# Opening SyncE's queue with wq and the K chunks, and loading x from ScalarE's queue, in a decode kernel of cached attention and a token mixer

## The chip, the cores and the metric

The kernel runs on one core of one Trainium2 chip. The core has TensorE (PE in the profile, with PEld for its weight loads), VectorE (DVE), ScalarE (ACT), GpSimd (POOL) and SyncE (SP), which here does nothing but issue DMAs. The metric is the device time of one execution in microseconds; less is better.

## The reference

Two layers, each a block of grouped-query attention over a cache and a token-mixing MLP, both with a residual. There are 2 batch rows with one token each and 512 channels; 32 query heads share 8 heads of keys and values, each with a cache of 32768 positions of 128 floats. Cut to what matters:

```python
def _A_ref(x, k_cache, v_cache, wq, wo):
    q = (x @ wq).reshape(B, Sq, Hq, Dh).transpose(0, 2, 1, 3)
    scores = jnp.einsum("bhqd,bhkd->bhqk", q, jnp.repeat(k_cache, rep, axis=1)) * (Dh ** -0.5)
    p = softmax(scores)
    o = jnp.einsum("bhqk,bhkd->bhqd", p, jnp.repeat(v_cache, rep, axis=1))
    return o.transpose(0, 2, 1, 3).reshape(B, Sq, Hq * Dh) @ wo

def _B_ref(x, w1, b1, w2, b2):           # S = 1 token, F = 1792
    u = gelu(jnp.einsum("bsd,sf->bdf", x, w1) + b1)     # x is layernormed again inside
    return jnp.einsum("bdf,fs->bds", u, w2) + b2

x = A_x
for _ in range(2):                        # the same weights and caches in both layers
    x = x + _A_ref(layernorm(x), k_cache, v_cache, wq, wo)
    x = x + _B_ref(layernorm(x), w1, b1, w2, b2)
```

All is float32. The caches are 2 x 8 x 32768 x 128 floats each for K and V, 268 MB each, and both layers read them whole.

## The kernel before, in words

The work is cut into 32 units: a layer, a batch row and one of the 8 heads of the cache. A unit reads its part of K and then of V in 8 chunks each; a chunk is a tile of 128 partitions by 4096 floats, 2 MB. All chunks, of K (`k_chunk`, L180) and of V (`v_chunk`, L247), are loaded from SyncE's queue into one ring of three buffers (`ring`, tile `chunk`). A load is issued as soon as the instructions that read the buffer's last content are done.

The order of the program is written out by hand (`manual_schedule`): a loop over slots (L412) that in each slot issues one chunk of K of a unit and one chunk of V of the unit before, and around them the small steps that two dictionaries, `pre` and `post`, assign to slots. Each engine runs its own instructions in that order, and each queue issues its DMAs in that order.

A unit's steps:

- `make_q` (L162): 16 products of a 128x128 block of wq with a column of the layernormed x (`xnT`); VectorE copies the four query vectors into `qpad`.
- `k_chunk`: scores of a chunk, 8 products with 512 positions each (L193; in float32 each counts as two matmuls in the profile); after each fourth chunk VectorE transposes the scores and takes the maximum.
- `max_1`, `max_2`: the maximum over the unit, and exp on ScalarE (L232).
- `v_chunk`: products of the weights with V, accumulated in `acc` (L270).
- `out_1`, `out_2`: sum, division, and the products with wo, added into `rows`.

After the last unit of a layer and a row come the mixer (`mix_2`, `mix_3`, `mix_3_out`) and `mix_4`, which adds to `xrow` and, in the last layer, issues the output row from ScalarE's queue (L366). `cols_sb` holds w1, b1, w2 and b2; the mixer alone reads it.

What concerns the change is the start. VectorE clears the tile `xrow` (L66), whose partitions 0 and 32 then receive the two rows of x (L68), 2 KB each. wq and wo are cut by head into 8 tiles each of 1 MB; `load_wq(0)` (L78, the DMA itself in L73) comes before the loop, the others in slots of the loop: wq of head 1 in slot 2, behind the third K chunk. From ScalarE's queue `cols_sb` is loaded (L80). Then VectorE and GpSimd prepare constants (VectorE: `selg`, `acc`, `rows`; L95 to L107). Before the loop stand the steps of the first unit: `attention_input` (L138) layernorms `xrow` with VectorE and GpSimd (L114 to L118), `to_columns` (L144) turns each row into columns by products with the identity (L149) and copies (L153), and `make_q(0, r)` forms the first q (L168, L176). Then the loop begins with chunk 0 of K. The chunks 0, 1 and 2 find empty buffers; chunk 3 takes the buffer of chunk 0.

Of the kernel before, what the change touches and what calls it, by code (L numbers as in the profile page):

```python
# [8 lines left out]
F32 = mybir.dt.float32  # L9
# [4 lines left out]
P = 128  # L14
# [16 lines left out]
def gqa_mixer_kernel(ctx: ExitStack, tc: tile.TileContext, x, kt, v, wq, wo, cols, out):  # L31
# [9 lines left out]
    nc = tc.nc  # L41
    B, D = x.shape
# [12 lines left out]
    const = ctx.enter_context(tc.tile_pool(name="const", bufs=1))  # L55
# [6 lines left out]
    ctx.enter_context(tc.manual_schedule())  # L62


    xrow = const.tile([P, D], F32, name="xrow")
    nc.vector.memset(xrow, 0.0)  # L66
    for b in range(B):
        nc.sync.dma_start(xrow[32 * b : 32 * b + 1, :], x[b : b + 1, :])  # L68
    wq_sb = [const.tile([P, DT, R * DH], F32, name=f"wq{h}") for h in range(HKV)]
    wo_sb = [const.tile([P, R, D], F32, name=f"wo{h}") for h in range(HKV)]  # L70

    def load_wq(h):
        nc.sync.dma_start(wq_sb[h].rearrange("p t c -> p (t c)"), wq[h])  # L73
# [2 lines left out]
        nc.sync.dma_start(wo_sb[h].rearrange("p t c -> p (t c)"), wo[h])  # L76

    load_wq(0)  # L78
    cols_sb = const.tile([P, 3 * FT + 1], F32, name="cols_sb")
    nc.scalar.dma_start(cols_sb, cols)  # L80
    w1c, b1c, w2c = (cols_sb[:, k * FT : (k + 1) * FT] for k in range(3))
# [74 lines left out]
    def unit_of(n):  # L156

        return units[n]
# [217 lines left out]
    for n in range(NU):  # L376
        layer, b, h = unit_of(n)
# [93 lines left out]
```

## Time and profile before

| | us |
|---|---|
| median of 3 runs | 2580.58 (2580.49 to 2580.9) |
| profiled execution | 2582.35 |
| its span, first to last instruction | 2580.6 |
| PE busy | 1676.7 (65%) |
| DVE busy | 224.1 (9%) |
| ACT busy | 135.3 (5%) |

In all 1085.71 MB move, at a mean of 421 GB/s over the span; 1084.27 MB of them belong to q1, the queue of SyncE. q10 is ScalarE's. TensorE was granted 0.788 of its clock in the mean.

In the views that follow, a row of the timeline has the start, the time that the instructions took, the engine (SPq and ACTq are the queues of SyncE and ScalarE that issue DMAs), the line and the operation, and behind them what ended an idle time before. A row of windows has, for each stretch, its length, the busy time and count of instructions of PE, PEld, DVE, ACT and POOL, then the granted clock of TensorE, the mean busy share of the 16 DMA engines and the GB/s. A row of a DMA queue has the number of packets, the MB and the share of the 16 engines' time. A row of DMA issues has the size of each transfer and the time from issue to landing.

### The profile page before, as it was taken

To read this page: it belongs to the slowest core of one execution; us is meant where nothing else is said; L and a number is where in the kernel's file an instruction comes from. 1 tells how busy PE (TensorE), PEld (TensorE's weight loads), DVE (VectorE), ACT (ScalarE), POOL (GpSimd) and SP (SyncE) were. 2 spreads that over 40 slices of the span, in tenths; PEclk is the share of its full clock that TensorE was granted. 3 is DMA by queue.
4 is the path that set the end of the run, shared out by engine and by line. 5 is a ranking of instruction groups with operands and counts; after the bars stand their busy time and mean duration, and the time that the engine had idled before them with its cause. 6 is when DMAs were issued, how large, how long until landed. Compare 5 with 4: busy or idle time off the path is not lost.

```text
span 2580.6 us, 22231 instructions
## 1 busy us (share of the span) xinstructions
PE 1676.7 (65%) x10088; PEld 488.4 (19%) x10088; DVE 224.1 (9%) x473; ACT 135.3 (5%) x280; POOL 7.0 (0%) x21
## 2 busy tenths in 40 slices
PE   6565666566676666765765666667667667667655
PEld 3111112121211221211211211212212212112111
DVE  1000000000021000000000000002001100000002
ACT  0000000000010000000000000001000100000001
POOL 0000000000000000000000000000000000000000
PEclk8877777777787778788778788878787877777887
DMA  9999999999999999999999999999999999999995
GB/s 404 428 427 427 428 426 428 426 427 425 427 427 426 423 426 421 427 428 427 427 426 427 425 428 425 427 426 428 425 428 421 426 428 427 428 427 425 428 428 220
DMA packets 76710, 1085.71 MB, mean 421 GB/s; under 512 B 8644, under 2 KB 8644, under 8 KB 9032
## 3 DMA queue, kind: packets, MB, share of 16 engines
q1 hardware_dynamic: 76468, 1084.27, 99.1%
q8 instruction: 79, 1.29, 0.2%
q14 instruction: 15, 0.12, 0.0%
q10 hardware_dynamic: 148, 0.03, 0.0%
HBM read 1084.25 MB, written 0.00 MB: 420 GB/s over the span
## 4 chain that ended last, share of the span: by engine, by line
DMA 77%; PE 22%; DVE 1%; issue 1%; ACT 0%; POOL 0%; POOLq 0%; SPq 0%; DVEq 0%; ACTq 0%
DMA chunk<-in_kt_dram 39%; DMA chunk<-in_v_dram 38%; PE acc L270 10%; PE scores L193 10%; PE misc L168 1%; PE misc L284 0%; PE rows L299 0%; DVE chunk L335 0%; PE rows L350 0%; PE misc L149 0%; PE misc L282 0%; ACT chunk L343 0%; ACT S L232 0%; DVE ln_st L114 0%; PE bcast L318 0%
## 5 line engine op out<-in xcount | busy, mean ns | idle before, releaser
L193 PE MATMUL scores<-chunk,qpad 128*32 128x512 f32 x4096 | 687.4, 803 | 457.5 <-DMA chunk<-in_kt_dram 455.0
L270 PE MATMUL acc<-chunk,S 128*16 128x512 f32 x4000 | 679.8, 811 | 421.8 <-DMA chunk<-in_v_dram 419.7
L193 PEld LDWEIGHTS scores<-chunk,qpad 128*32 128x32 f32 x4096 | 133.2, 128 | 887.5 <-DMA chunk<-in_kt_dram 452.5
L270 PEld LDWEIGHTS acc<-chunk,S 128*16 128x16 f32 x4000 | 109.1, 110 | 843.0 <-DMA chunk<-in_v_dram 586.1
L232 ACT ACTIVATE S<-S,neg 128x256 f32<-128x256 f32 x128 | 95.3, 749 | 2257.9 <-DVE neg L228 2257.9
L168 PEld LDWEIGHTS misc<-xnT,wq 128*128 128x128 f32 x1024 | 152.9, 230 | 157.9 <-issue 157.9
L168 PE MATMUL misc<-xnT,wq 128*128 128x1 f32 x1024 | 163.4, 281 | 0.0
L204 DVE STREAM_TRANSPOSE S<-scores 128x512 f32<-128x512 f32 x64 | 45.9, 717 | 845.6 <-PE scores L193 845.6
L176 DVE COPY qpad<-misc 128x4 f32<-128x4 f32 x32 | 5.2, 162 | 796.0 <-PE misc L168 796.0
L205 DVE TENSOR_REDUCE mx<-S 128x4 f32<-128x512 f32 x64 | 67.9, 1061 | 2.2
L284 PE MATMUL misc<-selg,row 128*128 128x4 f32 x256 | 42.2, 288 | 1.0 <-DVE row L280 1.0
L284 PEld LDWEIGHTS misc<-selg,row 128*128 128x128 f32 x256 | 40.7, 241 | 1.2 <-DVE row L280 1.2
L299 PE MATMUL rows<-wo,oT 128*1 128x512 f32 x256 | 40.0, 695 | 0.5 <-DVE oT L294 0.5
L220 DVE TENSOR_REDUCE m<-misc 4x1 f32<-4x128 f32 x32 | 8.9, 279 | 241.3 <-PE misc L218 241.3
L343 ACT ACTIVATE hid<-hid 128x2048 f32<-128x2048 f32 (+1 forms) x12 | 20.4, 1697 | 119.0 <-DVE hid L335 119.0
L280 DVE COPY row<-acc 128x512 f32<-128x512 f32 x32 | 21.8, 680 | 36.4 <-PE acc L270 36.4
L335 DVE TENSOR_SCALAR hid<-row,cols_sb 128x512 f32<-128x512 f32 x42 | 20.2, 541 | 53.4 <-PE rows L350 53.4
L232 ACT ACTIVATION_READ_ACCUMULATOR S<-S,neg 128x1 f32 x128 | 23.9, 187 | 0.0
L292 DVE RECIPROCAL rl<-misc 128x4 f32<-128x4 f32 x32 | 5.8, 182 | 170.9 <-PE misc L284 170.9
L282 PEld LDWEIGHTS misc<-lsum,one 128*128 128x128 f32 x64 | 12.3, 241 | 42.2 <-issue 42.2
L270 PE MATMUL acc<-kept,S 128*16 128x512 f32 x96 | 17.2, 840 | 2.1 <-DMA kept<-in_v_dram 2.1
L224 PEld LDWEIGHTS misc<-ident,m 4*128 4x128 f32 x64 | 11.2, 217 | 39.2 <-issue 38.3
(50 smaller groups left out, 193.6 us busy)
## 6 DMA issues: line engine op xcount, KB each, us to landing
chunk<-in_kt_dram SPq DMA_DIRECT2D x256, 2048.0 KB, 12.1
chunk<-in_v_dram SPq DMA_DIRECT2D x247, 2048.0 KB, 12.6
wq<-in_wq_dram SPq DMA_DIRECT2D x8, 1024.0 KB, 15.4
wo<-in_wo_dram SPq DMA_DIRECT2D x8, 1024.0 KB, 14.8
chunk<-in_v_dram SPq DMA_DIRECT2D x5, 1024.0 KB, 10.2
kept<-in_v_dram SPq DMA_DIRECT2D x2, 2048.0 KB, 16.4
kept<-in_v_dram SPq DMA_DIRECT2D x2, 1024.0 KB, 13.9
chunk<-in_v_dram SPq DMA_DIRECT2D x1, 512.0 KB, 11.1
```

The source lines that it names most:

```text
L168: nc.tensor.matmul(q_ps[n][:, r : r + 1], wq_sb[h][:, d, r * DH : (r + 1) * DH], xnT[layer, b][:, d : d + 1], start=(d == 0), stop=(d == D ...
L193: nc.tensor.matmul(sc_ps[n][32 * g : 32 * g + 32, :], q, kc[:, (k * NG + g) * w : (k * NG + g + 1) * w], start=(i == 0 and k == 0), stop=( ...
L204: nc.vector.transpose(S[n][:, half, :], sc_ps[n])
L205: nc.vector.tensor_reduce(mx[n][:, half, :], S[n][:, half, :].rearrange("p (t h) -> p h t", h=R), axis=AX.X, op=ALU.max,)
L232: nc.scalar.activation(s[:, :, h], s[:, :, h], AF.Exp, bias=neg[:, h : h + 1], scale=SCALE, accum_out=lsum[n][:, h : h + 1],)
L270: nc.tensor.matmul(acc[32 * g : 32 * g + R * QT, :], S[n][:, half, col : col + R * QT], (own if q < stay else vc)[:, q * w : (q + 1) * w], ...
L280: nc.vector.tensor_copy(asb, acc)
L282: nc.tensor.matmul(po[:, R : 2 * R], ones, lsum[n], start=True, stop=True)
L284: nc.tensor.matmul(po[:, :R], asb[:, t * DH : (t + 1) * DH], selg[:, t * R : (t + 1) * R], start=(t == 0), stop=(t == QT - 1),)
L299: nc.tensor.matmul(rows[b][32 * r : 32 * r + 1, :], oT[n][:, r : r + 1], wo_sb[h][:, r, :], start=(units[n] == lay[layer, b][0]), stop=(un ...
L335: nc.vector.tensor_scalar(u[:, k * D : (k + 1) * D], hx[key], w1c[:, f : f + 1], b1c[:, f : f + 1], op0=ALU.mult, op1=ALU.add,)
L343: nc.scalar.activation(u[:, : n * D], u[:, : n * D], AF.Gelu_apprx_tanh)
```

## The change

The two tile lists and the two loading functions move up, so that `load_wq(0)` is the first DMA in SyncE's order. The memset of `xrow` keeps its place on VectorE. The two rows of x are issued from ScalarE's queue, ahead of `cols_sb`. SyncE's queue then holds wq of head 0, the K chunks 0, 1 and 2, wq of head 1 and chunk 3, with no transfer of x among them. Sizes, tiles and all else stay.

```diff
+    wq_sb = [const.tile([P, DT, R * DH], F32, name=f"wq{h}") for h in range(HKV)]
+    wo_sb = [const.tile([P, R, D], F32, name=f"wo{h}") for h in range(HKV)]
+
+    def load_wq(h):
+        nc.sync.dma_start(wq_sb[h].rearrange("p t c -> p (t c)"), wq[h])
+
+    def load_wo(h):
+        nc.sync.dma_start(wo_sb[h].rearrange("p t c -> p (t c)"), wo[h])
+
+    load_wq(0)
     xrow = const.tile([P, D], F32, name="xrow")
     nc.vector.memset(xrow, 0.0)
     for b in range(B):
-        nc.sync.dma_start(xrow[32 * b : 32 * b + 1, :], x[b : b + 1, :])
-    wq_sb = [const.tile([P, DT, R * DH], F32, name=f"wq{h}") for h in range(HKV)]
-    wo_sb = [const.tile([P, R, D], F32, name=f"wo{h}") for h in range(HKV)]
...
-    load_wq(0)
+        nc.scalar.dma_start(xrow[32 * b : 32 * b + 1, :], x[b : b + 1, :])
     cols_sb = const.tile([P, 3 * FT + 1], F32, name="cols_sb")
     nc.scalar.dma_start(cols_sb, cols)
```

More of the change, by code (lines that the diff above doesn't have):

```diff
@@ L62, in gqa_mixer_kernel @@
     ctx.enter_context(tc.manual_schedule())
[L65 to L68, printed above, removed]
     wq_sb = [const.tile([P, DT, R * DH], F32, name=f"wq{h}") for h in range(HKV)]
@@ L78, in gqa_mixer_kernel @@
     load_wq(0)
+    xrow = const.tile([P, D], F32, name="xrow")
+    nc.vector.memset(xrow, 0.0)
+    for b in range(B):
+        nc.scalar.dma_start(xrow[32 * b : 32 * b + 1, :], x[b : b + 1, :])
     cols_sb = const.tile([P, 3 * FT + 1], F32, name="cols_sb")
```

## The prediction

> **What bounds the kernel now.** I read the page from the top: the span, the busy shares, the row of the DMA in 40 slices, then the chain that ended last.
>
> ```profile
> span 2580.6 us, 22231 instructions
> PE 1676.7 (65%) x10088; PEld 488.4 (19%) x10088; DVE 224.1 (9%) x473; ACT 135.3 (5%) x280; POOL 7.0 (0%) x21
> DMA  9999999999999999999999999999999999999995
> DMA 77%; PE 22%; DVE 1%; issue 1%; ACT 0%; POOL 0%; POOLq 0%; SPq 0%; DVEq 0%; ACTq 0%
> ```
>
> The DMA is at nine tenths or more in 39 of 40 slices and carries 77% of the chain; the busiest engine, PE, has 65%. To see whether the DMA ever rests, I cut the span in three windows. The last two columns are the DMA's busy share and GB/s.
>
> ```profile
> 0.00:3.00 3.00, 0.00 (x0) 0.00 (x0) 1.84 (x5) 1.28 (x1) 0.95 (x10) 1.00 0.06 9
> 3.00:2550.00 2547.00, 1660.65 (x10024) 484.86 (x10028) 209.13 (x441) 126.13 (x274) 4.95 (x9) 0.79 1.01 426
> 2550.00:2580.60 30.60, 16.08 (x68) 3.58 (x60) 13.15 (x28) 7.85 (x5) 1.10 (x2) 0.76 0.02 6
> ```
>
> From 3 to 2550 us the transfers run without rest (share 1.01, 426 GB/s). So the kernel is a dead start of 3 us, a stream of fixed length, and a serial tail of 30 us. A microsecond gained or lost where the stream starts is kept to the end, because no slack lies in the stream that could swallow it. A change that touches only the start has to be read in the first 25 us, in SyncE's queue first.
>
> ```profile
> SPq L68 <- DVE xrow L66: 0.7, 1, 0.7
> ...
> 1.43 0.63 SPq L68 DMA_DIRECT2D xrow<-in_x_dram  x2
> 2.11 0.35 SPq L73 DMA_DIRECT2D wq<-in_wq_dram  x1
> 2.50 1.66 SPq L184 DMA_DIRECT2D chunk<-in_kt_dram  x3
> 4.21 0.45 SPq L73 DMA_DIRECT2D wq<-in_wq_dram  x1
> 20.04 3.97 SPq L184 DMA_DIRECT2D chunk<-in_kt_dram  x3
> ```
>
> SyncE waits 0.7 us for VectorE's memset of xrow (L66), spends 0.63 us on the two rows of x and issues wq at 2.11. After three K chunks and the second wq the ring of three buffers is full, and the fourth chunk goes out at 20.04, when PE has read the first. That PE work hangs on x:
>
> ```profile
> 0.74 0.39 ACTq L80 DMA_DIRECT2D cols_sb<-in_cols_dram  x1
> 0.91 0.48 DVE L66 MEMSET xrow<- 128x512 f32 x1 [0.91 <-PEq L457]
> 1.17 1.28 ACT L232 ACT_TABLE_LOAD   x1 [1.17 <-PEq L457]
> 2.34 1.03 DVE L107 MEMSET rows<- 128x512 f32 x2
> 3.29 0.69 DVE L114 BATCH_NORM_STATS2 ln_st<-xrow 128x6 f32<-128x512 f32 x1
> 9.17 6.97 PE L168 MATMUL misc<-xnT,wq 128*128 128x1 f32 x32
> 16.17 0.16 DVE L176 COPY qpad<-misc 128x4 f32<-128x4 f32 x1 [6.66 <-PE misc L168]
> 16.43 7.19 PE L193 MATMUL scores<-chunk,qpad 128*32 128x512 f32 x48 [0.30 <-issue]
> ```
>
> x, layernorm, columns, q, scores are one serial line from 3.29 to 20.04, with no wait for a transfer in it before the third chunk. So there are two clocks at the start: when the stream begins, and when x's line frees the first buffer. The change moves the first earlier and perhaps the second later.
>
> **The change, part by part.**
>
> *SyncE's queue opens with wq.* Its first DMA no longer waits for the memset nor stands behind the two issues of x. The wait of 0.7 us ended at 1.43, so SyncE was ready at 0.73; ScalarE's first issue at 0.74 shows the same start. wq moves from 2.11 to 0.74, and the three chunks and the second wq with it: the stream begins 1.37 us earlier. That is −1.37 us at the end if nothing runs dry.
>
> *x on ScalarE's queue.* The issue still waits for the memset (0.91 plus 0.48), so it begins at 1.43 as before. Behind it on ScalarE stand cols and the table load. cols goes out about 1.3 us later and the table load ends near 3.8 instead of 2.45. They are covered, and I take them at nothing:
>
> ```profile
> 60.06 0.77 ACT L232 ACTIVATE S<-S,neg 128x256 f32<-128x256 f32 x1 [57.61 <-DVE neg L228]
> 749.06 0.99 DVE L335 TENSOR_SCALAR hid<-row,cols_sb 128x512 f32<-128x512 f32 x2
> ```
>
> The table is first used at 60.06 and cols at 749.06; without that cover they would cost at most the 1.3 us each.
>
> *x now travels beside the stream.* Before, it went ahead of wq on idle DMA engines. Its last packet, the completion write of the second row, is the one packet of q1 in the window 2.8 to 3.0 us:
>
> ```profile
> q1 hardware_dynamic: 1, 0.00, 0.3%
> ```
>
> VectorE was busy with memsets until just before 3.29, so x may land 0.3 us later for nothing. How late it lands under load is seen nowhere at the start; the nearest rows are those of the first output row, also 2 KB, also from ScalarE's queue, in the full stream. The fence gives ScalarE's issue, SyncE's own issues around it, the landing of the chunk issued just ahead of it (11.0 us), and the packets of queue q10 in the windows 2039.65 to 2039.75 and 2040.35 to 2040.45, and of q1 in the 0.6 us between:
>
> ```profile
> 2036.19 0.49 ACTq L366 DMA_DIRECT2D out_dram<-xrow  x1
> ...
> 2033.67 0.33 SPq L261 DMA_DIRECT2D chunk<-in_v_dram  x1
> 2036.93 0.33 SPq L184 DMA_DIRECT2D chunk<-in_kt_dram  x1
> ...
> chunk<-in_v_dram SPq DMA_DIRECT2D x1, 2048.0 KB, 11.0
> ...
> q10 hardware_dynamic: 1, 0.00, 5.4%
> ...
> q1 hardware_dynamic: 16, 0.26, 102.3%
> ...
> q10 hardware_dynamic: 1, 0.00, 0.6%
> ```
>
> The row's data moved 3.5 us after its issue and its completion write 4.2 us after. It didn't wait for the chunk issued at 2033.67, which landed at 2044.7: it got between that chunk's packets. Sixteen engines moved sixteen packets of 16 KB in the 0.6 us between its two packets, one each. So a small transfer here waits some microseconds and then takes turns one for one.
>
> Unloaded, x's second row took 1.2 us (issue near 1.8, done by 3.0), so load adds 3.0 us. Lower end for the start: nothing, as the engines' first packets move only from about 1.7 on. Upper end: 1.8 + 4.2 = 6.0 for the second row, plus two turns of 0.7 if the first row's two packets go ahead: 7.4. My value lies between: the engines then carry wq's packets of 8 KB, half a chunk's, so I take half of 3.0, giving 2.9 + 1.5, and one turn of half length (0.35) for the first row: 4.75. ScalarE's issue may cost 0.49 rather than 0.35; that is within the ends. VectorE's statistics start at 4.7 instead of 3.29. Call this delay d: 1.4 us, ends 0 and 4.1.
>
> The Trainium skill's page "DMA: Bandwidth & Descriptors", section "Queues, rings and completion order", says that each engine round-robins between queues packet by packet, but that a packet typically holds 9 to 17 descriptors. By that, a turn would cost about a whole load's share of one engine, and the sum would be +4.2 to +5.0 us (the third rival). The turn of 0.7 us in the rows above speaks against the long turn.
>
> *Does the stream run dry before the fourth chunk?* These rows are the first windows of the stream, the bytes that q1 had moved by 23.24, and wq's first packets in the window 3.0 to 3.25:
>
> ```profile
> 2.00:3.00 1.00, 0.00 (x0) 0.00 (x0) 0.89 (x3) 0.45 (x1) 0.00 (x0) 1.00 0.06 10
> 3.00:4.00 1.00, 0.00 (x0) 0.00 (x0) 0.99 (x2) 0.00 (x0) 0.00 (x0) 1.00 0.79 139
> 4.00:5.00 1.00, 0.00 (x0) 0.00 (x0) 0.34 (x2) 0.00 (x0) 0.45 (x1) 1.00 0.88 369
> 5.00:6.00 1.00, 0.26 (x2) 0.26 (x2) 0.55 (x1) 0.00 (x0) 0.10 (x1) 1.00 1.05 442
> ...
> q1 hardware_dynamic: 705, 8.37, 95.1%
> ...
> q1 hardware_dynamic: 8, 0.07, 215.2%
> ```
>
> Two wq (1.05 MB each) and three chunks (2.10 MB each) are 8.39 MB: the backlog ends at about 23.24, and in the changed kernel at 21.87. The fourth chunk's issue comes at 20.04 + d. From issue to data the only unloaded row is wq itself: issued 2.11, first packets in 3.0 to 3.25, so 1.0 us. Counted in bytes it is more: 139 + 369 + 442 = 950 KB by 6.0, which at 442 GB/s is 2.15 us of full flow, as if it had begun at 3.85, 1.74 us after the issue. So the fourth chunk is in time as long as d stays under s = 21.87 − 20.04 − 1.0 = 0.83, or, with the slow filling, 0.09. Beyond that each microsecond of d is a hole in the stream.
>
> **The sum:** −1.37 + (d − s), and never under −1.37. With d = 1.4: −1.37 + 0.57 = −0.80 to −1.37 + 1.31 = −0.06; I take the middle, −0.4 us. The profiled execution took 2582.35 us, 1.75 more than its span and 1.77 over the median; it becomes 2581.95, and the median 2580.58 becomes 2580.2. The 0.2% about what a measurement of this kernel can tell from no change is 5.2 us; everything above lies inside it.
>
> **Rivals.**
> - *x is not held up* (d within s): x lands by about 3.3 to 4.1 and the full 1.37 us stays: 2579.2. For it: at 1.43 the engines have hardly begun. Against it: by 2.3, when x's packets are due, wq's have begun at 1.7 and fill the engines.
> - *x waits as the output row did*, d up to 4.1: the hole is 3.3 to 4.0 us and the sum +1.9 to +2.6: 2582.5 to 2583.2. The same rows speak for it; against it, the half-sized packets of wq.
> - *Slower: x waits behind whole loads.* If an engine finishes its share of a load before it turns, the first row goes after wq and the second after the first chunk. That is 3.15 MB, reached near 11 us before (950 KB at 6.0, then 442 GB/s) and 9.6 now: d = 6.4, sum +4.2 to +5.0, so 2584.8 to 2585.6. If x stands behind all that SyncE has issued by 2.0, the second chunk too (4.9 us more), the sum is about +9 to +10, 2589.5 to 2590.5, beyond 0.2%. It decides from d of about 2 us. Against both: the output row overtook a chunk issued 2.5 us before it. For them: at the start five loads are queued within 2.6 us, more than the output row met.
> - *The change does less than it says*: SyncE isn't ready at 0.74, or the table load goes ahead of x on ScalarE (1.17 to 2.45), which adds 0.6 to 1.0 us to d: the sum goes from −0.4 to between +0.2 and +0.6, up to 2581.2.
>
> **How the numbers follow.** My forecast 0.50, hidden 0.17, the long wait 0.14, whole loads 0.10 (half of it in its longer form), less than it says 0.03, and 0.06 for a stream of another rate, either way. The range 2579.0 to 2583.3 takes in the first three and the fifth, 0.84; its low end is the hidden case less half the spread of the runs (0.4 us). Slower by over 0.2%: 0.05 for the longer form and 0.03 for another rate; faster: 0.03, as only another rate could do it (0.2% of 426 GB/s). Same: the other 0.89.
>
> **What would show it.** SyncE's wq at 0.74 and no wait at L68; ScalarE's two x issues at 1.43; the statistics at about 4.7; the fourth chunk's issue at about 21.4; a dip in the DMA's share at 22 to 23 us; from there the same stream, ending at 2550 within a microsecond. Statistics at 3.3 mean the hidden case, at 7 the long wait, at 9 or later whole loads. The forecast fails if x is held for more than about 6 us, or if the stream's rate differs from 426 GB/s.

## The result, and the profile after

The changed kernel takes 2585.82 us in the median of 14 runs (2582.87 to 2587.58), the kernel before 2581.41 (2580.07 to 2584.31). The ratio is 1.0015, with a 95% interval of 1.0008 to 1.0022: slower by 4.4 us, or by 2.1 to 5.7 us. That is within the 0.2% of "same", but it lies above the forecast's range (2583.3) and on the other side of its 0.4 us gain. The profiled execution took 2587.04 us, with a span of 2585.3.

The page after has the same shape: the span, the DMA row in 40 slices, and the shares of the chain.

```profile
span 2585.3 us, 22231 instructions
DMA  9999999999999999999999999999999999999995
DMA 75%; PE 23%; DVE 1%; issue 1%; ACT 0%; POOL 0%; POOLq 0%; ACTq 0%; DVEq 0%
```

Nothing here shows where 4.4 us went; the 40 slices are 65 us wide each. The first 30 us of the timeline do (the issues of SyncE and of x, the statistics of x, the first scores):

```profile
0.74 0.38 SPq L69 DMA_DIRECT2D wq<-in_wq_dram  x1
1.18 1.63 SPq L184 DMA_DIRECT2D chunk<-in_kt_dram  x3
1.43 0.76 ACTq L78 DMA_DIRECT2D xrow<-in_x_dram  x2
8.32 0.69 DVE L114 BATCH_NORM_STATS2 ln_st<-xrow 128x6 f32<-128x512 f32 x1 [4.96 <-DMA xrow<-in_x_dram]
21.47 7.51 PE L193 MATMUL scores<-chunk,qpad 128*32 128x512 f32 x48 [0.30 <-issue]
25.16 14.98 SPq L184 DMA_DIRECT2D chunk<-in_kt_dram  x5
```

wq left at 0.74, 1.37 us earlier, as forecast, and x was issued at 1.43, as forecast. But VectorE then sat idle for 4.96 us on x, and its statistics began at 8.32 instead of 3.29: the delay d is 5.0 us. All of x's line moved with it, down to the fourth chunk's issue, 25.16 instead of 20.04. Meanwhile the backlog of the stream was used up. These are windows of the changed kernel; the last two columns are the DMA's share and GB/s.

```profile
20.00:22.00 2.00, 1.70 (x10) 1.31 (x14) 0.16 (x1) 0.00 (x0) 0.00 (x0) 1.00 1.02 430
22.00:24.00 2.00, 2.00 (x12) 0.45 (x8) 0.00 (x0) 0.00 (x0) 0.00 (x0) 1.00 0.08 33
24.00:26.00 2.00, 2.00 (x16) 0.66 (x12) 0.00 (x0) 0.00 (x0) 0.00 (x0) 1.00 0.03 8
26.00:28.00 2.00, 2.00 (x24) 0.61 (x20) 0.00 (x0) 0.00 (x0) 0.00 (x0) 1.00 0.88 238
```

From 22 to 26 us the 16 engines moved almost nothing (33 and 8 GB/s), and refilled slowly. To price it I count what SyncE's queue had moved by 100 us, first before, then after:

```profile
q1 hardware_dynamic: 3112, 41.23, 97.5%
```

```profile
q1 hardware_dynamic: 3000, 39.72, 94.2%
```

1.51 MB less is 3.5 us at the 427 GB/s that most of the page's 40 slices show. By 300 us the two have moved 126.57 and 125.05 MB, 1.52 apart: in this stretch the loss neither grows nor heals. So 3.5 us of the 4.4 belong to the first 30 us. In this pair of profiles the span differs by 4.7 us, 1.2 more than that, and most of it sits in one place; the windows from 990 to 1040 us, before and then after:

```profile
990.00:1040.00 50.00, 33.73 (x221) 11.81 (x225) 3.50 (x9) 3.05 (x8) 0.00 (x0) 0.83 1.01 425
```

```profile
990.00:1040.00 50.00, 38.10 (x212) 11.55 (x204) 3.12 (x7) 3.05 (x8) 0.00 (x0) 0.67 0.99 411
```

TensorE was granted 0.67 of its clock there instead of 0.83, and the stream lost 14 GB/s for 50 us: the gap between the two kernels grows from 1.31 to 2.04 MB, by 1.7 us, and stands at 1.99 MB at 2500 us. The changed kernel run once more (below) loses 0.17 MB there, at 422 GB/s; I take this loss as an accident of one execution; its cause is not shown.

### The profile page after: what moved, and what is told of

It is laid out like the page before. It is cut to its first block, busy times and chain, and to the rows that moved or that the text cites. A ratio compares the mean times of both kernels' runs of the same rounds, so it can differ in the third digit from the quotient of the medians.

```text
span 2585.3 us, 22231 instructions
## 1 busy us (share of the span) xinstructions
PE 1681.2 (65%) x10088; PEld 483.0 (19%) x10088; DVE 224.0 (9%) x473; ACT 135.4 (5%) x280; POOL 7.0 (0%) x21
## 4 chain that ended last, share of the span: by engine, by line
DMA 75%; PE 23%; DVE 1%; issue 1%; ACT 0%; POOL 0%; POOLq 0%; ACTq 0%; DVEq 0%
DMA chunk<-in_kt_dram 39%; DMA chunk<-in_v_dram 36%; PE scores L193 11%; PE acc L270 10%; PE misc L168 1%; PE misc L284 0%; PE rows L299 0%; DMA xrow<-in_x_dram 0%; PE rows L350 0%; PE misc L149 0%; DVE chunk L335 0%; PE misc L282 0%; ACT chunk L343 0%; ACT S L232 0%; DVE ln_st L114 0%
## 5 line engine op out<-in xcount | busy, mean ns | idle before, releaser
L193 PE MATMUL scores<-chunk,qpad 128*32 128x512 f32 x4096 | 705.7, 823 | 470.5 <-DMA chunk<-in_kt_dram 468.0
L168 PE MATMUL misc<-xnT,wq 128*128 128x1 f32 x1024 | 158.2, 276 | 0.0
L228 DVE TENSOR_SCALAR neg<-misc 128x4 f32<-128x4 f32 x32 | 5.2, 162 | 127.9 <-PE misc L224 127.9
```

What stands on the lines that cost most here:

```text
L168: nc.tensor.matmul(q_ps[n][:, r : r + 1], wq_sb[h][:, d, r * DH : (r + 1) * DH], xnT[layer, b][:, d : d + 1], start=(d == 0), stop=(d == D ...
L193: nc.tensor.matmul(sc_ps[n][32 * g : 32 * g + 32, :], q, kc[:, (k * NG + g) * w : (k * NG + g + 1) * w], start=(i == 0 and k == 0), stop=( ...
```

## The experiments

In every table and text below, "behind" is the difference in MB by 100 us to the 41.23 MB above, divided by 427 GB/s; the medians are of 11 runs each, beside 33 of the kernel before on the same chip. The runs of one kernel spread over 3 to 7 us, and the 95% interval of a ratio is some 2.3 us wide to either side, so a total tells nothing smaller; what tells the kernels apart is the traces' first 30 us. "Theory A", "theory B" and "theory C" are named in the expectations, which stand ahead of each result as they were written.

**The line alone made late.** The kernel before, with x and wq as they were:

```diff
+    for _ in range(10):
+        nc.vector.memset(acc, 0.0)
     h0 = attention_input()
```

> The kernel before with ten more memsets of acc on VectorE ahead of the first layernorm (about 0.5 us each); nothing else is moved, x and wq leave as before. Theory A (what costs time is that x's line, layernorm to scores, ends 5 us later, so the fourth K chunk is issued near 25.2 us and the stream runs dry): the stream's start is as before, but the fourth chunk's data come at the same time as in the changed kernel, so the total is that of the changed kernel, +3.5 to +4.5 us on before. Theory B (the loss comes from ScalarE's queue or from the small transfers disturbing the stream): the line has slack and the total moves by +2.0 us at most.

The memsets took 0.67 us each with their waits. wq left at 2.11 as before. The statistics, the fourth chunk's issue and the bytes by 100 us:

```profile
9.81 0.64 DVE L114 BATCH_NORM_STATS2 ln_st<-xrow 128x6 f32<-128x512 f32 x1
26.59 3.21 SPq L184 DMA_DIRECT2D chunk<-in_kt_dram  x2
q1 hardware_dynamic: 2964, 39.06, 93.2%
```

The line is 6.5 us late, not 5, the fourth chunk is issued at 26.59, and the stream is 2.17 MB, 5.1 us, behind; the median is 2586.51 against 2582.34 (ratio 1.0015, 1.0006 to 1.0024). The issue is 1.4 us later than in the changed kernel and the loss 1.5 us greater, as theory A has it. No transfer was moved here: a late line is enough. Theory B isn't needed, and the next run, in which x comes late from ScalarE's queue and the stream loses nothing, takes it away.

**A fourth buffer.** The changed kernel, with the fourth chunk of the first unit in the tile `kept`, idle at that time (its allocation moves up in the program):

```diff
-        kc = ring.tile([P, CK], F32, name="chunk")
+        if n == 0 and c == RING:
+            kc = kept[:, :CK]
+        else:
+            kc = ring.tile([P, CK], F32, name="chunk")
```

> The changed kernel, with the fourth K chunk of the first unit loaded into the tile kept, which is idle until the end of the first layer's first row; so it waits for no buffer and is issued behind the second wq near 3.3 us. Theory A: x is as late as in the changed kernel (statistics at 8.3 us), but the stream has 4.9 us more in its backlog, until 26.8 us, and the fifth chunk's issue near 25.2 comes in time: no dry stretch, and the total is 1.4 us under before (-1.0 to -1.6). Theory B (disturbance of the stream itself): still slower than before by 2 us or more.

```profile
8.20 0.70 DVE L114 BATCH_NORM_STATS2 ln_st<-xrow 128x6 f32<-128x512 f32 x1 [4.84 <-DMA xrow<-in_x_dram]
22.00:24.00 2.00, 2.00 (x16) 0.56 (x12) 0.00 (x0) 0.00 (x0) 0.00 (x0) 1.00 0.99 418
24.00:26.00 2.00, 2.00 (x16) 0.55 (x12) 0.00 (x0) 0.00 (x0) 0.00 (x0) 1.00 1.13 483
q1 hardware_dynamic: 3133, 41.63, 98.7%
```

The fourth chunk is issued at 5.70, not near 3.3 as I expected: SyncE waited 2.3 us for wq to land. That is still long before the backlog ends. x is as late as in the change (8.20), but the two windows that were empty now run at 418 and 483 GB/s, and the stream is 0.40 MB, 0.9 us, ahead, where I expected 1.4. The median is 2580.74 against 2582.34 (0.9992, 0.9983 to 1.0001). So x's lateness costs nothing while the backlog lasts.

The same kernel once more:

> The changed kernel with the fourth K chunk in the idle tile kept, once more, to narrow its interval: the bytes moved by 100 us are 0.4 MB ahead of the kernel before (1.0 us), and the total is 1.0 us under it (-0.3 to -1.6).

Again 41.63 MB by 100 us; 2580.76 against 2582.03 (0.9998, 0.9989 to 1.0006). It is the best kernel of the study by its stream and by its medians (1.3 to 1.6 us; the two ratios give 0.5 and 2.1), but neither interval is clear of 1, and I don't call it faster.

**The fourth buffer without the change**, as its control:

> The kernel before with the fourth K chunk in the tile kept, nothing else. Its stream never ran dry at the start, so a fourth buffer there has nothing to cover: bytes by 100 us as before (41.2 MB), total 0 (-0.5 to +0.5). If the fourth buffer helped by itself, the gain of the changed kernel with it could not be put down to the earlier start.

```profile
q1 hardware_dynamic: 3093, 40.92, 97.0%
```

0.31 MB, 0.7 us, behind, where I had expected none; the median is 2581.72 against 2582.03 (0.9998, 0.9989 to 1.0007). By 40 us the two kernels stand level (15.60 and 15.59 MB), so the buffer brings nothing at the start; the loss falls between 40 and 60 us, where the first V chunk goes out at 55.23 instead of 53.01, and I didn't follow it further. The 0.9 us that the stream gains with the fourth buffer above is thus the earlier start, not the buffer.

**The change once more**, beside the first three:

> The changed kernel once more, beside the others on the same chip, as the measure for them: +3.5 to +4.8 us on before.

```profile
8.04 0.69 DVE L114 BATCH_NORM_STATS2 ln_st<-xrow 128x6 f32<-128x512 f32 x1 [4.68 <-DMA xrow<-in_x_dram]
24.81 3.76 SPq L184 DMA_DIRECT2D chunk<-in_kt_dram  x3
q1 hardware_dynamic: 3005, 39.80, 94.7%
```

3.3 us behind; 2585.43 against 2582.34, +3.1 us (1.0011, 1.0002 to 1.0019), a little under the 3.5 to 4.8 that I expected.

**x issued at 0.74**, each row copied to 32 partitions so that it needs no memset:

```diff
-    nc.vector.memset(xrow, 0.0)
+    nc.vector.memset(xrow[32 * B :, :], 0.0)
     for b in range(B):
-        nc.scalar.dma_start(xrow[32 * b : 32 * b + 1, :], x[b : b + 1, :])
+        nc.scalar.dma_start(xrow[32 * b : 32 * b + 32, :], x[b : b + 1, :].to_broadcast([32, D]))
```

> The changed kernel, with each row of x copied by its load to 32 partitions, so that partitions 0 to 63 need no memset and ScalarE issues both loads at 0.74 us, with wq's load and not behind the first chunks. Theory A: x's packets reach the engines before or with wq's first ones, the statistics start between 3.3 and 4.5 us, the fourth chunk is issued by 21.3, and the total is -1.4 to 0 us against before. Rival (a small transfer beside the stream always waits some 4 us from its issue, whenever it is issued): statistics at 6 to 7.5 us, total +1.5 to +3.

The issues and the statistics, and ScalarE's queue (q10) in the windows 2 to 3, 3 to 4 and 5 to 6 us; from 4 to 5 it has no packet:

```profile
0.73 0.89 ACTq L78 DMA_DIRECT2D xrow<-in_x_dram  x2
8.20 0.69 DVE L114 BATCH_NORM_STATS2 ln_st<-xrow 128x6 f32<-128x512 f32 x1 [4.85 <-DMA xrow<-in_x_dram]
25.04 3.79 SPq L184 DMA_DIRECT2D chunk<-in_kt_dram  x3
q10 hardware_dynamic: 12, 0.02, 6.3%
q10 hardware_dynamic: 36, 0.04, 11.4%
q10 hardware_dynamic: 13, 0.03, 6.9%
```

The copies make the rows visible one by one. 48 packets are through by 4 us, the whole first row: issued at 0.73, with wq, it went in among wq's first packets. The second row, issued some 0.45 us later (1.18), is the one that starts in the window 5 to 6, near 5.45, and holds x until 8.20. So theory A's number fails, and the rival falls with the first row, which did not wait 4 us: what a small transfer pays here depends on whether SyncE's load has a lead over it. Total 2584.59 against 2582.34 (1.0007, 0.9998 to 1.0016); 3.5 us behind.

**ScalarE's queue without wq's lead.** SyncE first loads one more copy of a row, to a partition that nothing uses, behind the memset; then wq:

```diff
-    load_wq(0)
 ...
         nc.scalar.dma_start(xrow[32 * b : 32 * b + 1, :], x[b : b + 1, :])
+    nc.sync.dma_start(xrow[64:65, :], x[0:1, :])
+    load_wq(0)
```

> The changed kernel with x still on ScalarE's queue, but SyncE first issues a copy of x's first row to partition 64, which nothing uses; that load waits for the memset, so wq leaves near 1.8 us, with the second row of x and not before it. Theory C (a row of x that ScalarE issues before the first K chunk goes in among wq's packets; one issued after it waits until the engine has finished its share of wq, and one K packet more): both rows arrive near 4 us, statistics at 3.3 to 4.6 us, the fourth chunk at 20.0 to 21.4 us, no dry stretch, total -0.3 us against before (-0.8 to +0.3). Rival (ScalarE's queue is slow beside SyncE's whatever the order): statistics near 8 us, total +3 or more.

```profile
1.43 0.76 ACTq L77 DMA_DIRECT2D xrow<-in_x_dram  x2
1.83 0.35 SPq L69 DMA_DIRECT2D wq<-in_wq_dram  x1
4.42 0.69 DVE L115 BATCH_NORM_STATS2 ln_st<-xrow 128x6 f32<-128x512 f32 x1 [1.05 <-DMA xrow<-in_x_dram]
21.26 4.19 SPq L185 DMA_DIRECT2D chunk<-in_kt_dram  x3
q1 hardware_dynamic: 3110, 41.23, 97.3%
```

The statistics start at 4.42, 3.9 us sooner than in the changed kernel, though x was issued at the same time from the same queue. The stream stands where it stood before (41.23 MB). x on ScalarE's queue, with wq issued 0.4 us behind its first row, costs 1.1 us, which the backlog covers; the lead of SyncE's loads over x costs the rest. The median, 2584.06 against 2581.76 (1.0006, 0.9997 to 1.0015), is 2.3 us up all the same, with single runs from 2580.45 to 2586.63; the interval holds 1, the profiled execution is the fastest of the 11, and I read nothing from it; the −0.3 us that I expected is not shown.

**wq ahead, x on SyncE's queue:**

```diff
-        nc.scalar.dma_start(xrow[32 * b : 32 * b + 1, :], x[b : b + 1, :])
+        nc.sync.dma_start(xrow[32 * b : 32 * b + 1, :], x[b : b + 1, :])
```

> SyncE's queue opens with wq, but the two rows of x follow on the same queue, and the K chunks behind them. Theory C: x has to let wq's share go first but takes no turns with K, so its rows land near 5.5 us, the statistics start at 5.4 to 6.0, the fourth chunk is issued near 22.3 us, and the total is +0.7 us against before (0 to +1.5). If only the leaving of ScalarE's queue mattered, the statistics would start at 3.3 and the total be -1.4.

```profile
6.28 0.69 DVE L114 BATCH_NORM_STATS2 ln_st<-xrow 128x6 f32<-128x512 f32 x1 [2.92 <-DMA xrow<-in_x_dram]
23.01 3.76 SPq L184 DMA_DIRECT2D chunk<-in_kt_dram  x3
q1 hardware_dynamic: 3075, 40.62, 96.5%
```

Statistics at 6.28, 0.61 MB or 1.4 us behind, 2583.7 against 2581.76 (1.0005, 0.9996 to 1.0014). Of the 5.0 us, then, 3.0 come from standing behind wq at all, and 2.0 more with ScalarE's queue; the next run says what most of these 2.0 are.

**Both rows in one load:**

```diff
-    for b in range(B):
-        nc.scalar.dma_start(xrow[32 * b : 32 * b + 1, :], x[b : b + 1, :])
+    nc.scalar.dma_start(xrow[0 : 32 * B : 32, :], x)
```

> The changed kernel with both rows of x in one load from ScalarE's queue, to partitions 0 and 32. Theory C: it still waits for wq's share and one K packet (data at 5.7 us), but the second row no longer takes two turns of its own (1.3 us): statistics at 7.0 us, the fourth chunk at 23.9, 1.0 MB behind at 100 us (2.4 us). If the rows' turns don't matter: 8.2 us, 25.0 and 1.5 MB as in the changed kernel.

```profile
6.70 0.69 DVE L113 BATCH_NORM_STATS2 ln_st<-xrow 128x6 f32<-128x512 f32 x1 [3.34 <-DMA xrow<-in_x_dram]
23.53 4.75 SPq L183 DMA_DIRECT2D chunk<-in_kt_dram  x3
q1 hardware_dynamic: 3044, 40.24, 96.0%
```

The second row's own turns are worth 1.3 to 1.6 us (6.70 against 8.04 and 8.32), so that ScalarE's queue without them costs 0.4 us against the run before (6.70 against 6.28). The stream is 2.3 us behind, as expected. 2584.81 against 2582.03 (1.0008, 0.9999 to 1.0017).

**A K chunk ahead of wq**, to see what the wait is made of:

```diff
+    first = ring.tile([P, CK], F32, name="chunk")
+    nc.sync.dma_start(first, kt[0, 0])
     load_wq(0)
...
+        if n == 0 and c == 0:
+            kc = first
+        else:
```

> The changed kernel with the first K chunk (2 MB) ahead of wq (1 MB) in SyncE's queue; x from ScalarE's queue as in the change. Theory C (x waits until the engine is through its share of the load in front): the share now is eight packets of 16 KB, 4.9 us, and x's first packet comes near 7.5 us instead of 5.7; turns with wq's packets are shorter, statistics near 9.1 us, the fourth chunk near 25.9, 1.9 MB behind at 100 us (4.4 us). Rival (a wait of fixed length, or of a fixed number of bytes): first packet at 5 to 6 us, statistics at 7.5 to 8.3.

The landing of the load issued at 0.74 (the K chunk), ScalarE's queue in the window 5.6 to 5.95 (x's first row, and one packet of cols), what SyncE's queue had begun to move by 5.8, and the statistics, the issue and the bytes as above; in the second fence the first two of the changed kernel, where the load in front is wq.

```profile
chunk<-in_kt_dram SPq DMA_DIRECT2D x1, 2048.0 KB, 7.8
q10 hardware_dynamic: 2, 0.00, 1.8%
q1 hardware_dynamic: 82, 1.34, 68.6%
8.25 0.69 DVE L116 BATCH_NORM_STATS2 ln_st<-xrow 128x6 f32<-128x512 f32 x1 [4.89 <-DMA xrow<-in_x_dram]
25.09 4.76 SPq L189 DMA_DIRECT2D chunk<-in_kt_dram  x3
q1 hardware_dynamic: 2996, 39.65, 95.1%
```

```profile
wq<-in_wq_dram SPq DMA_DIRECT2D x1, 1024.0 KB, 4.9
q10 hardware_dynamic: 1, 0.00, 1.5%
```

In the changed kernel x's first row moves just after wq has landed (5.6), and it looks as if it had waited for the whole load. With the chunk in front it moves at the same time, 5.8, though only 82 of the chunk's 128 packets have begun by then, the first completion write of the chunk comes at 7.28, and the chunk lands only at 8.5. Theory C falls: the wait isn't the share of the load in front but 4.4 us from the issue, in both (4.2 in the change's second profile). A fixed number of packets it isn't either: 158 of wq and the chunk behind it had begun in the changed kernel. Whether it is a time, a number of bytes (1.34 and 1.54 MB had begun) or goes by the loads issued ahead of x (the same two in both kernels) these runs don't tell. The stream is 3.7 us behind; the median 2587.44 against 2582.03 (1.0021, 1.0012 to 1.0030) is 1.7 us worse than that, a difference that I can't place.

**Both rows at 0.74, ahead of wq**, one from each queue:

```diff
-    load_wq(0)
     xrow = const.tile([P, D], F32, name="xrow")
-    nc.vector.memset(xrow, 0.0)
+    nc.vector.memset(xrow[32 * B :, :], 0.0)
     for b in range(B):
-        nc.scalar.dma_start(xrow[32 * b : 32 * b + 1, :], x[b : b + 1, :])
+        (nc.scalar, nc.sync)[b].dma_start(xrow[32 * b : 32 * b + 32, :], x[b : b + 1, :].to_broadcast([32, D]))
+    load_wq(0)
```

> Both rows of x leave at once near 0.74 us without waiting for a memset (each copied to 32 partitions): row 0 from ScalarE's queue, row 1 from SyncE's ahead of wq, which leaves near 1.1 us. Theory C: both rows are ahead of wq's share, statistics at 3.3 to 3.6 us, the stream starts 1.0 us earlier than before, no dry stretch: -1.0 us (-0.6 to -1.4). If small transfers always wait, statistics near 5 us or later and total 0 or more.

```profile
1.18 0.41 SPq L69 DMA_DIRECT2D wq<-in_wq_dram  x1
3.37 0.69 DVE L114 BATCH_NORM_STATS2 ln_st<-xrow 128x6 f32<-128x512 f32 x1
q1 hardware_dynamic: 3173, 41.57, 98.6%
```

x is in time. Less the copies of a row that this queue carries (0.06 MB more), the stream is 0.28 MB or 0.7 us ahead, short of the 1.0 expected, and the total shows nothing: 2582.09 against 2581.76 (1.0003, 0.9994 to 1.0012).

**The wait for the memset alone.** The kernel before with the same copies, x first on SyncE's queue:

> The kernel before, x on SyncE's queue ahead of wq, but without the wait for the memset (each row copied to 32 partitions). The stream starts as much earlier as the wait was long, 0.7 us; x lands by 2.5 us, statistics at 3.3 us as VectorE is busy till then, the fourth chunk at 20.0: total -0.7 us against before (-0.3 to -1.0).

```profile
0.74 0.86 SPq L68 DMA_DIRECT2D xrow<-in_x_dram  x2
1.65 0.42 SPq L73 DMA_DIRECT2D wq<-in_wq_dram  x1
q1 hardware_dynamic: 3205, 41.37, 98.2%
```

The two copying loads took 0.86 us to issue instead of 0.63, so wq left 0.46 us earlier, not 0.7; less the 0.13 MB of copies the stream is level with before, and so is the total (2581.6 against 2581.76; 0.9997, 0.9988 to 1.0006). That expectation failed: the time won at the issue isn't found in the stream. The copies are 0.13 MB, or 0.3 us of it; that they took the rest as well is not shown.

**All together.** Sorted by the fourth chunk's issue, the kernels without a fourth buffer in which it came after 21 us:

| kernel | fourth chunk issued, us | behind at 100 us, us |
|---|---|---|
| ScalarE's queue without wq's lead | 21.26 | 0.0 |
| wq ahead, x on SyncE | 23.01 | 1.4 |
| both rows in one load | 23.53 | 2.3 |
| the change once more | 24.81 | 3.3 |
| x issued at 0.74 | 25.04 | 3.5 |
| a K chunk ahead of wq | 25.09 | 3.7 |
| the change | 25.16 | 3.5 |
| the line alone late | 26.59 | 5.1 |

From about 21.5 us on, a microsecond there is about a microsecond of the stream, whatever made it late, and whether the stream had begun at 1.8 us or, as in the last row, at 3.1: once it has run dry its earlier start is forgotten. The 21.5 agrees with the prediction's backlog in the kernel before, to 23.24, less its 1.74 us of slow filling.

## Why the prediction was wrong

*What bounds, and where to look:* right. The loss lies in the first 30 us and is kept.

*The earlier start of SyncE's queue, −1.37 us:* right in the issue (0.74), too large in the stream. The lead in bytes is 0.62 MB (1.4 us) at 6 us, but 0.44 MB (1.0 us) at 10 and 0.38 MB (0.9 us) at 20, before anything ran dry, and with the fourth buffer 0.9 us, twice, at 100. Between 6 and 10 us x's rows and packets of cols move amid the stream; that these took the 0.4 us is not shown.

*cols and the table load at nothing:* nothing contradicts it in x's line; the statistics wait for x alone. Whether cols, now amid the stream, takes a little of its lead is the open point above.

*The delay d of x:* this is the step that failed. I had 1.4 us, with ends of 0 and 4.1; it is 5.0. Three terms were too small. I halved the wait that the output row showed because wq's packets are half as long; the run with a K chunk in front shows the same wait with packets twice as long, and at 4.2 to 4.4 us from the issue it was even longer than the output row's 3.5. The turn of the second row I took at 0.35; it is 1.3 to 1.6 in all. And I ended x's time at its completion write, which comes at 7.84 in the changed kernel, 0.48 us before the statistics; in the kernel before, 0.42 us lay between the two (2.87 and 3.29), so of the 0.3 us that I had granted x for nothing hardly any were there. The chain of the changed kernel, in order of time, puts 6.2 us between the issue of the second row and VectorE:

```profile
1.97 6.23 DMA xrow<-in_x_dram
```

The nearest row of the trace was at hand, and taken whole it gave d = 4.1, 0.9 short; I used it as an end, and took a middle that no row showed.

*The hole, d − s:* the form was right. With d = 5.0 my sum gives 2.8 to 3.6 us, and 3.5 was measured; the end of s with slow filling (0.09) is the right one. The middle of the two was no better founded than that of d. The earlier start stands in the sum twice, as −1.37 and within s, and cancels once the stream runs dry; so its being too large did no harm.

*The rivals:* the long wait (+1.9 to +2.6) was the right case with its end set too low. Whole loads (+4.2 to +5.0) hit the total of 4.4 us by its number, though the statistics came at 8.32 and not at 9 or later; that was luck. The run with the K chunk in front takes its mechanism away, and with it the long turn that I had drawn from the Trainium skill's page "DMA: Bandwidth & Descriptors" ("Queues, rings and completion order"): x got in amid a load's share, at 82 of its 128 packets. The hidden case fell. "SyncE isn't ready" fell too.

*The spread:* I took the low end from a spread of 0.4 us in three runs. Fourteen runs of the kernel before spread over 4.2 us, with a median 0.8 us above that of the three, and the chance of 0.03 for a drift in the stream was optimistic for single runs, as the window near 1000 us shows.

## What to carry to other kernels

Where transfers never rest, look at the start for two clocks: when the stream begins, and when the first buffer comes free; an earlier start is worth only what the second clock leaves of it. A small load on which a serial line hangs belongs ahead of the bulk, also when it goes out from another queue; here a lead of 0.7 us for the bulk cost x's line 3.9 us against the run in which wq had none. For an unknown wait use the nearest row whole rather than a middle between it and nothing, and count it as far as the engine that waits.

## What the runs showed of the hardware that I had not expected

- A 2 KB load issued from ScalarE's queue with wq and a K chunk already issued ahead of it by SyncE moved 4.2 to 4.4 us after its issue, with packets of 8 KB and of 16 KB in front alike. A row issued together with the first bulk load, copied to 32 partitions, was through between 2.5 and 4 us, the second one, issued 0.45 us later, began near 5.45.
- The second row, in a load of its own behind the first, took 1.3 to 1.6 us more.
- A stream that has run dry refills slowly: in the changed kernel the fourth chunk was issued at 25.16, and the window from 26 to 28 us moved 238 GB/s at a share of 0.88.
- Loads that copy a row to 32 partitions took longer to issue (0.86 us for two, against 0.63).
